# Turned rows as plain f32 matmuls, no folded row pairs, new instruction orders

## The chip, the core and the metric

The kernel runs on one core of one Trainium2 chip. The metric is device time of one execution in microseconds (us); the figure given is the median of three runs. The core's engines work at the same time and wait for each other by semaphores: TensorE (PE, matrix products, with its weight loads PEld), VectorE (DVE), ScalarE (ACT), GpSimd (POOL) and SyncE (SP, which here only issues DMAs). TensorE writes to PSUM, which has eight banks of 2 KB per partition; VectorE and ScalarE fetch results from there.

## What is computed

The input x has 2048 rows and 512 columns in bf16. Two layers with the same weights follow each other. Each adds a spectral filter, then a mixer with an MLP, both on normed rows:

```python
def _A_ref(x, w_r, w_i):
    X = rfft2(x);  X = X * (w_r + 1j * w_i);  return irfft2(X)
def _B_ref(x, w1, w2, w3, w4):
    h = gelu(layernorm(x) @ w1)
    # the four column quarters of h, shifted by +1, -1, +2, -2 rows
    x1 = x + concatenate([g0, g1, g2, g3]) @ w2
    return x1 + gelu(layernorm(x1) @ w3) @ w4

for _ in range(2):
    x = x + _A_ref(layernorm(x), A_w_r, A_w_i)
    x = x + _B_ref(layernorm(x), B_w1, B_w2, B_w3, B_w4)
return x
```

w1 and w2 are 512x512, w3 512x1792, w4 1792x512.

## The kernel before

x stays in on-chip memory as 16 tiles of 128x512, here called rows 0 to 15 (row q holds the rows p*16 + q of x, p being the partition). The transform over 2048 is split into one over p (128 points) and one over q (16 points); the transform over the 512 columns is another. All of them are matmuls with constant tables. Much of the work is in pairs of rows.

The order in which instructions are issued is written out by hand in three strings: ORDER_0 for the first front, ORDER_A and ORDER_B for the two layers. A token is one letter for an operation, a number, perhaps the engine that does it (A, V, P for ScalarE, VectorE, GpSimd; D is a product done by VectorE straight from PSUM), and after a dot the PSUM bank where its result begins. Every engine runs its own instructions in the order of the strings, and what stands behind a waiting instruction waits too. The steps that matter here:

- **First front** (ORDER_0). `s`: statistics of a row, on VectorE (one instruction), or for rows 1, 5 and 9 on ScalarE (two). `i`: their aggregate. `f`: the remaining arithmetic for a row that ScalarE did, on GpSimd; `f2` also issues four table loads (FL, TL twice, TR) from GpSimd's queue. `S` and `J`: root and reciprocal of the deviation for a group of rows, on ScalarE and VectorE. `Q`: the table T scaled by a row's factor. `O`: the transform over p of a pair of rows. `G`, `L`, `I`: fetching its result into V. After the last of them GpSimd copies the doubled planes of the filter W and makes a turned table.
- **Layer, spectral part.** `d`: transform over the columns, from all of V; `t` fetches it. `q`: transform over q; `x` fetches it; `p` multiplies with the filter. `b` (and `V`): back over q; `m` and `l` fetch into hT. `N`: VectorE negates a part of the table TR. `D` and `C`: back over the columns for a pair of rows m, into two banks; `Y` fetches a pair as bf16 (128x1024). `P`: back over p for one row; `a` adds it to x and sums the row.
- **Layer, norm and turn.** `s` squares (ScalarE), `r`, `e`, `i`, `M` make the factors, `n` norms a row (ScalarE, VectorE or GpSimd). `T` (and `U` for the second norm) turns a pair of rows with TensorE; `Z` (and `F`) fetches the turned rows into xT. `v`: product with w1; `h` its gelu; `u`: with w2; `f` the residual. `w`, `g`, `W`, `A`: product with w3, gelu, product with w4, addition. The second layer ends with stores `y`; the first runs the next front (`O` and what belongs to it) between its last products.
- `X`: a number of matmuls on zeros that nobody reads; `fill` makes them.

FOLD names row pairs whose way back over p is halved. For pairs 4 to 7 (rows 8 to 15), `K` fetches the right halves of the pair's result to f32, `H` (fold_D, line 670) makes sum and difference with the left halves on VectorE, and P then needs two matmuls of 256 columns (line 678) for the four (line 683) of the other rows:

```python
if q // 2 in FOLD[last]:
    for h in range(2):                                # 2 matmuls
        ...
for h, e, c in ((0, 0, 0), (0, 1, 0), (1, 0, 0), (1, 1, 1)):   # 4 matmuls
```

A turn writes eight transposes of 128x128 as bf16 into one bank, and the copy (line 154 on ScalarE, 152 on VectorE) fetches 128x1024 bf16.

Of the kernel before, what the change touches and what calls it, by code (L numbers as in the profile page):

```python
# [148 lines left out]

def copy(K, dst, src, eng):  # L150
    if eng == "V":
        K.nc.vector.tensor_copy(dst, src)
    else:
        K.nc.scalar.activation(dst, src, ACT.Copy, bias=0.0, scale=1.0)  # L154
# [406 lines left out]
def layer(K, last):  # L561
# [143 lines left out]

    def turn(key, rows):

        ps[key] = o = banks(K, 1)[:, 0].bitcast(BF16).rearrange("p (i t c) -> p i t c", i=2, t=4)
        for i in range(2):
            for t in range(4):  # L710
                nc.tensor.transpose(o[:, i, t], rows[:, i, t * P:(t + 1) * P], K.unit[:])  # L711
# [194 lines left out]
ORDER_A = """
d0.0 d2.4 t2A d6.2 d1.1 N0 t0V t6A t1V q0.6 q2.4 x2A d4.0 t4A q6.2 p0D q1.6 x1A d10.4 p2V d12.0 t10A t12A d8.6 q4.4
t8A q10.0 x10A p6D b6.2 m6A b2.7 d14.6 b7.3 q8.0 m2A p4D b4.4 t14A b5.2 x8A d15.5 q14.6 q12.0 m7A p10V b11.3 m5A t15A
m4A b3.2 p1V x14A b1.5 m1A b10.4 m10A p8V p12D q15.6 b8.5 m11A b9.4 b12.0 b13.1 m8A b0.3 p15D V12.5 m9A m12A b15.4 m3A
p14V m15A b14.7 m14A m13V V13.0 V14.1 V15.4 m0V l14V l13A l12V D2.6 D0.0 l15A C2 C0 Y0A D1.2 C1 D3.4 Y1A C3 P0.0 P1.2  # L910
Y2V Y3A P3.1 P2.3 P7.4 a0 s0 a1 s1 P6.0 a3 s3 D5.6 C5 P4.1 a2 s2 K5A P5.5 D4.2 a6 s6 a7 a4 r0 e0 a5 C4 s7 K4A i0 M0
n2P n3A s4 D6.4 D7.0 C7 n0P H5 H4 n1V s5 T1.6 Z1A r1 e1 P11.7 P8.2 T0.3 a11 i1 M1 n4P a8 Z0A C6 P10.6 P9.7 n6A v1.2 h1
a9 n5P T2.7 a10 n7P T3.6 s11 v0.2 K6V H6 Z3V P12.6 Z2A v3.4 K7V c1 c0 s9 P13.7 H7 P15.0 P14.1 s10 s8 h3 h0 r2 v2.4 n9P
n8P a13 a14 u0.1 h2 a12 n11V u3.3 n10V a15 T5.5 s12 s14 f3 s13 T4.0 s15 r3 n15P Z5V u2.2 n14P u1.7 c3 f2 E2P Z4A v5.3
k3 v4.5 T7.0 f0 f1 k1 h5 u4.1 n13V h4 c2 u5.4 k0 n12V T6.5 Z6A u6.2 f5 Z7V u7.4 f6 v6.6 v7.2 E3V f4 k2 E5V h6 E1V h7
u14.7 R0 o1V o2A E6V E0V o0V u12.1 o3V k4 f14 f7 k6 U0.2 k14 U1.6 F1V u15.0 E4V f15 u9.3 F0A w4.4 u8.0 g4 u13.7 k5 E7V
k7 R1 o5P w0.4 f8 E8V k8 f12 k12 o7P k15 E14V f13 k13 w3.0 g3 u10.2 f10 E12V w2.6 g2 f9 g0 k9 w1.0 g1 u11.7 f11 w5.2
k11 E11V k10 R3 E15V g5 o12P o14P R2 E10V w6.5 o4A g6 W2.2 E13V o15P U7.4 o10P U2.3 W3.0 o11P o13A A2 B2 j2 U5.7 A3
o6P U3.2 W1.5 A1 B1 F3A U6.2 F6A F5V E9P F2A W0.0 o9V A0 w7.2 F7A B0 j0 o8P U4.0 g7 w10.4 g10 B3 w9.2 w8.4 g8 F4V j1
w13.0 g13 j3 w17.4 g17 w14.0 g14 S0 Q3V Q0P Q1P g9 O0.4 G0A w11.6 g11 w12.1 g12 W5.0 A5 G0V I0P Q2A O1.2 B5 j5 W7.6  # L920
W6.1 A7 W4.4 A6 w15.0 B6 j6 G1A w16.6 G1V g15 w25.0 w18.2 g18 g25 A4 B4 I1P g16 w20.4 w19.2 B7 j7 j4 g19 g20 W10.1 A10
B10 j10 W9.5 S1 Q7A Q5A Q4A O2.0 Q6P O3.2 G3A G3V W8.4 A8 B8 j8 A9 B9 W11.3 A11 B11 G2A w22.4 G2V I2V I3V w23.2 w21.0
j9 j11 S2 Q11P Q10P g22 w24.4 Q8A g24 Q9A w26.6 g23 g26 g21 w27.4 O5.2 G5A O4.6 g27 G5V I5V G4A W12.0 A12 B12 G4V j12
S12 W15.1 A15 B15 j15 S15 J15 Q15V I4V W13.6 W14.3 A13 W24.7 B13 J12 j13 S13 J13 O15.1 A14 A24 B14 B24 j14 Q12A Q13P
S14 O6.4 G6A G15A J14 Q14V O14.6 G14A L15V L14A L6V
"""
ORDER_B = """
d15.3 t15V d1.2 d4.4 d0.3 t0V t1A q1.0 q15.6 t4A d12.2 q4.4 p1D x15A q0.6 t12A x4A d2.1 t2A p15V p0D b15.0 d10.3 t10A
m15V q12.6 x12A q2.0 d8.2 t8A p4V d6.4 d14.6 b1.7 p2D q8.2 t6A q10.0 p12V b4.4 t14A q6.5 m1A x10A b0.7 p8D x6A b2.1
b5.0 b12.5 b8.3 b9.2 m4A m5A b3.6 m2A p6V b7.4 m0A q14.0 m8A p10V m3A b6.7 b13.3 m7A b10.6 b11.4 m12A m6A V15.5 m9V  # L930
p14D b14.2 V14.7 V12.0 m10A m11V V13.1 m13A l14V m14A D0.2 l15A l12A l13A D2.5 C2 Y2V D1.0 C1 C0 Y0V Y1A D3.4 C3 Y3A
P4.7 a4 P5.1 P2.2 a5 s4 P7.3 s5 P6.6 a7 s7 P0.1 a6 s6 a0 P3.0 s0 a3 D5.4 C5 K5A P1.3 a2 D4.6 C4 r1 e1 s2 a1 D7.0 C7 i1
H5 X6.2 P10.2 K4A H4 M1 n6P s1 n7A T3.3 s3 P11.4 Z3A n4V n5P T2.6 r0 a10 P9.5 a11 e0 i0 D6.2 a9 K7V M0 P8.7 a8 n3P C6
Z2A s10 v2.4 n2A H7 T1.6 s9 K6V Z1V n0P n1P T0.7 H6 s8 s11 r2 v3.0 n10V n8V Z0A v1.6 n11V P14.2 a14 P13.3 a13 h3 T5.0
c0 P12.1 h2 h1 v0.4 P15.2 Z5V h0 u1.0 a12 n9V a15 T4.6 s12 Z4V u0.4 s14 f1 E1V s15 c1 s13 r3 n12P u2.5 f2 k2 f0 v4.2
v5.0 n15P u3.6 k1 n13A h4 n14V T7.7 f3 T6.2 h5 u4.3 k0 E3V E0V Z6V u5.6 Z7A f4 u7.1 v6.2 E2P k3 c2 f5 v7.6 f7 k7 h6 h7
u6.2 u13.0 f6 E7V R0 o1P o0A U0.1 F0V o2P u8.4 c3 f8 o3A U1.6 f13 E6P E13P E5V k6 k4 u9.5 f9 u14.4 F1A u15.0 f15 E9V
E4V f14 E14V k5 k8 R1 o4P u12.6 k13 w2.2 u11.7 f11 k9 g2 w4.0 k14 w1.2 w5.4 o7A k15 f12 w0.6 k12 R3 o14P o6V o13P g5
E11V g1 g4 w3.4 g3 w6.0 g0 E15V o15A u10.2 f10 k10 E12P U3.4 o12V E10P g6 W2.5 k11 R2 o5V U7.0 o11V U6.3 F6A o9P E8V
A2 W1.1 A1 F7A w23.6 w24.0 o8A U4.5 U2.2 F3A w27.3 g23 w22.6 F4A g24 F2V y2 w21.0 g22 o10P w25.6 g21 U5.2 F5V W0.1 g27  # L940
W3.0 A0 g25 w26.2 g26 W12.4 w8.6 W15.5 A3 w7.0 g7 A12 A15 W14.2 A14 w15.3 y0 W13.2 A13 w19.0 g15 g19 w20.4 w18.0 w13.2
g18 y1 g20 w16.0 g16 w14.4 y15 g8 g14 w17.0 w9.4 g9 w12.6 w10.4 g12 y3 g10 y12 y13 g13 w11.6 g11 W4.5 A4 y4 W7.3 W5.2
A7 y14 W6.6 A6 A5 y7 y5 y6 g17 W8.0 W11.6 A8 y8 A11 y11 W9.4 W10.3 A9 y9 A10 y10 W20.2 A20 y20
"""


# [28 lines left out]
```

## Time and profile before

| | |
|---|---|
| median of three runs | 357.88 us (357.71 to 357.96) |
| profiled execution: its own time, and its span | 357.88 us, 356.1 us |
| TensorE busy | 347.6 us in 2408 matmuls |
| VectorE, ScalarE, GpSimd busy | 181.6, 208.7, 102.7 us |
| first front: first product, last product | 8.48, 18.86 us |
| first layer: first D, first w1 | 37.93, 51.74 us |
| second layer: first d, first D, first w1 | 189.2, 207.34, 221.23 us |
| last product with w4 ends | 352.9 us |

Times in the profile are counted from the start of the span. Busy time of TensorE counts a matmul from start to modelled end, and matmuls overlap by their latency; so the step from one start to the next in a stream says what one costs. "Idle before" is the time that an engine stood still before the instructions of a group, with what ended it. In the chain that ended last, each piece is what the next one waited for.

### The profile page before, as it was taken

The numbers are of one execution on the slowest core, as the hardware profiler recorded it, in microseconds if no ns is written. First come the engines' busy times: TensorE is split into PE (matmuls) and PEld (weight loads), VectorE is DVE, ScalarE is ACT, GpSimd is POOL, SyncE is SP. The second block draws the span as 40 slices with busy tenths as digits, with TensorE's granted clock in tenths as the row PEclk, the third lists the DMA queues.
The fourth block names the chain that finished last, engine by engine and source line by source line (L and its number), as shares of the span: only waits on it lengthen the run. The fifth ranks groups of instructions, "written<-read, shape, count | busy, mean of one in ns | idle before, by whom it ended". The sixth has DMA issues, their size and how long they took to land.

```text
span 356.1 us, 6134 instructions
## 1 busy us (share of the span) xinstructions
PE 347.6 (98%) x2408; PEld 198.5 (56%) x2408; DVE 181.6 (51%) x399; ACT 208.7 (59%) x381; POOL 102.7 (29%) x213
## 2 busy tenths in 40 slices
...
GB/s 255 305 303 172 346 174 0 2 1 3 0 2 0 0 2 0 0 2 0 2 0 2 3 3 0 3 0 2 0 1 17 0 29 31 28 3 2 44 44 47
DMA packets 11534, 16.25 MB, mean 46 GB/s; under 512 B 1344, under 2 KB 8512, under 8 KB 11504
## 3 DMA queue, kind: packets, MB, share of 16 engines
...
q14 instruction: 11, 0.09, 0.1%
q10 hardware_dynamic: 144, 0.07, 0.1%
...
## 4 chain that ended last, share of the span: by engine, by line
PE 88%; DVE 5%; ACT 3%; issue 1%; DMA 1%; SPq 0%; ACTq 0%; DVEq 0%
PE ps L799 27%; PE ps L779 27%; PE ps L728 8%; PE ps L744 8%; PE ps L635 4%; PE ps L711 4%; DVE x_state L691 3%; PE ps L424 3%; PE ps L655 2%; PE ps L587 1%; PE ps L605 1%; DMA x_state<-in_A_x_dram 1%; DVE Y L670 1%; ACT TV L154 1%; PE ps L434 1%
## 5 line engine op out<-in xcount | busy, mean ns | idle before, releaser
L779 PE MATMUL ps<-xT,w 128*128 128x512 bf16 x448 | 99.6, 379 | 0.0
L799 PE MATMUL ps<-w,gT 128*128 128x512 bf16 (+2 forms) x476 | 99.5, 366 | 0.0
L786 ACT ACTIVATE gT<-ps 128x1024 bf16<-128x1024 f32 x56 | 55.3, 1023 | 73.5 <-PE ps L779 66.7
L805 DVE TENSOR_TENSOR x_state<-ps,x_state 128x512 bf16<-128x512 f32 (+2 forms) x34 | 22.3, 659 | 101.4 <-PE ps L799 99.4
L799 PEld LDWEIGHTS <-gT 128*128 128x128 bf16 x476 | 45.2, 98 | 49.7 <-DVE pairs L456 0.2
L779 PEld LDWEIGHTS <-w 128*128 128x128 bf16 x448 | 43.7, 98 | 52.1
L752 DVE SCALAR_TENSOR_TENSOR xn<-xn,ln_c,ps 128x512 bf16<-128x512 bf16 x32 | 23.3, 744 | 27.5 <-PE ps L744 18.3
L744 PE MATMUL ps<-w,hT 128*128 128x512 bf16 x128 | 30.6, 379 | 0.0
L728 PE MATMUL ps<-xT,w 128*128 128x512 bf16 x128 | 29.4, 379 | 0.5 <-ACT xT L154 0.5
L154 ACT ACTIVATE xT<-ps 128x1024 bf16<-128x1024 bf16 x19 | 19.0, 1019 | 12.4 <-PE ps L711 12.4
L298 ACT ACTIVATE junk<-xn 128x512 bf16<-128x512 bf16 x32 | 19.9, 622 | 4.8 <-DVE xn L752 4.5
L691 DVE SCALAR_TENSOR_TENSOR x_state<-ps,x_state 128x512 bf16<-128x512 f32 x32 | 20.5, 684 | 3.0 <-PE ps L678 1.5
L286 DVE BATCH_NORM_STATS2 ln_st<-x_state 128x6 f32<-128x512 bf16 (+2 forms) x30 | 19.4, 665 | 4.3 <-DMA x_state<-in_A_x_dram 3.9
L728 PEld LDWEIGHTS <-w 128*128 128x128 bf16 x128 | 12.4, 98 | 14.4 <-issue 0.7
L304 POOL TENSOR_SCALAR ln_mv<-ln_s 128x4 f32<-128x4 f32 x16 | 4.1, 258 | 55.8 <-DVE x_state L691 49.1
L298 ACT ACTIVATE xn<-x_state 128x512 bf16<-128x512 bf16 x32 | 19.8, 622 | 0.3
L744 PEld LDWEIGHTS <-hT 128*128 128x128 bf16 x128 | 12.2, 98 | 13.0
L711 PEld LDWEIGHTS <-xn 128*128 128x128 bf16 x256 | 16.1, 98 | 5.6 <-ACT xn L397 0.6
L711 PE MATMUL ps<-unit,xn 128*128 128x128 bf16 x256 | 18.2, 219 | 0.5 <-ACT xn L397 0.3
L735 ACT ACTIVATE hT<-ps 128x512 bf16<-128x512 f32 x32 | 17.2, 602 | 2.4 <-PE ps L728 2.3
L621 DVE TENSOR_TENSOR PB<-ps,W 128x1024 bf16<-128x1024 f32 x15 | 17.7, 1216 | 0.0
L635 PE MATMUL ps<-TR,PB 128*128 128x128 bf16 x256 | 16.3, 219 | 0.1
...
## 6 DMA issues: line engine op xcount, KB each, us to landing
...
```

What stands on the lines that cost most here:

```text
L154: K.nc.scalar.activation(dst, src, ACT.Copy, bias=0.0, scale=1.0)
L298: K.nc.scalar.activation(out, src, ACT.Square, bias=0.0, scale=D ** -0.5, accum_out=self.s[:, i, 1:2])
L635: nc.tensor.matmul(o[:, k0 * P:(k0 + 1) * P], lhsT=pab[u][:, k, 2 * (b - u) + h, f * P:(f + 1) * P], rhs=K.TR[:, k:k + 2, 2 * b + h], star ...
L691: nc.vector.scalar_tensor_tensor(K.x[:, q, :], ps.pop(("P", q)), 1.0, K.x[:, q, :], op0=ALU.mult, op1=ALU.add, accum_out=ln[g].s[:, i, 0:1])
L711: nc.tensor.transpose(o[:, i, t], rows[:, i, t * P:(t + 1) * P], K.unit[:])
L728: nc.tensor.matmul(o[:, i], lhsT=K.w1[:, t, j * P:(j + 1) * P], rhs=xT[g][:, :, t, :], start=(t == 0), stop=(t == 3))
L744: nc.tensor.matmul(o, lhsT=K.hT[:, j, st:st + P], rhs=K.w2[:, j, :], start=(j == 0), stop=(j == 3))
L752: nc.vector.scalar_tensor_tensor(xn[:, q, :], xn[:, q, :], ln[q // 4].c[:, q % 4:q % 4 + 1], ps.pop(("u", n)), op0=ALU.mult, op1=ALU.add, ...
L779: nc.tensor.matmul(o[:, i], lhsT=K.w3[:, c, t * P:(t + 1) * P], rhs=xT3[g][:, :, c, :], start=(c == 0), stop=(c == 3))
L786: nc.scalar.activation(gT[g][:, 2 * j:2 * j + 2, :], ps.pop(("w", k)), ACT.Gelu_apprx_tanh, bias=0.0, scale=1.0)
L799: nc.tensor.matmul(o, lhsT=gT[g][:, t, i * P:(i + 1) * P], rhs=K.w4[:, t, d], start=(t == 0), stop=(t == 13))
L805: nc.vector.tensor_tensor(x, ps.pop(("W", n)), x, op=ALU.add)
```

## The change

Three things change; all else, the loads among them, stays as it was.

1. The turn is a plain matmul with the unit matrix as moving operand. Its result is f32 over two banks in place of bf16 in one; one copy per pair of rows fetches 128x1024 f32.
2. FOLD is empty: rows 8 to 15 take the four matmuls as the others do, `K` and `H` are gone, and `Y` fetches pairs 4 to 7.
3. All three orders are new.

```diff
     def turn(key, rows):
 
-        ps[key] = o = banks(K, 1)[:, 0].bitcast(BF16).rearrange("p (i t c) -> p i t c", i=2, t=4)
+        ps[key] = o = banks(K, 2)
         for i in range(2):
             for t in range(4):
-                nc.tensor.transpose(o[:, i, t], rows[:, i, t * P:(t + 1) * P], K.unit[:])
+                nc.tensor.matmul(o[:, i, t * P:(t + 1) * P], lhsT=rows[:, i, t * P:(t + 1) * P], rhs=K.unit[:],
+                                 start=True, stop=True)
...
-        copy(K, to[g][:, 2 * h:2 * h + 2], ps.pop(key), eng)
+        copy(K, to[g][:, 2 * h:2 * h + 2].rearrange("p q t c -> p q (t c)"), ps.pop(key), eng)
...
-FOLD = [(4, 5, 6, 7), (4, 5, 6, 7)]
+FOLD = [(), ()]
 ORDER_0 = """
-s0 s2 s1 f0 s3 i2 s5 f2 i0 S0 i3 S1 s7 J0 s6 Q0A s4 s9 J1 Q1V O0.5 Q2A i6 i4 i7 S2 s10 J2 Q3A s11 f3 Q4A Q5A s8 i11
-i10 i8 s12 G0A S3 J3 s15 Q7A s13 Q10A Q9V i13 Q6P O1.2 Q8V O2.0 O3.4 i15 G2A Q11P i12 G1A s14 S4 J4 G3A i14 Q12V Q13V
-S5 O5.6 L5A O4.0 J5 G3V Q14P G5A G4A O6.2 Q15V I3V O7.6 O8.4 G6A G7A G8A L7V L8A L6V
+s1 f0 s0 i0 s2 i2 s3 i3 s8 s5 S0 J0 S1 J1 s9 s10 i8 s11 Q2A Q3A O1.6 i10 Q1A s12 i11 Q0P s15 f3 S3 J3 Q10A i12 s13 s4
+Q11A i13 s7 i4 Q8A O0.1 G0A s6 i6 S4 G1A J4 Q12V i7 Q9P O5.3 f2 L5A s14 S2 J2 Q4V Q7V i15 Q13A O4.0 Q6P O6.6 i14 Q5P
+G5V G4A S5 J5 L6A Q14V O3.4 G3A G6A O2.0 G2A Q15V O8.2 G8A L8A G3V I3V O7.6 G7A L7V
 """
 ORDER_A = """
-d0.0 d2.4 t2A d6.2 d1.1 N0 t0V t6A t1V q0.6 q2.4 x2A ...
+X5.0 d1.0 d0.1 t0A d2.2 t2A d10.6 t10A N0 t1V q0.4 q1.0 p0D ...
...
-... D2.6 D0.0 l15A C2 C0 Y0A D1.2 C1 D3.4 Y1A C3 P0.0 P1.2
-Y2V Y3A P3.1 P2.3 P7.4 a0 s0 a1 s1 P6.0 a3 s3 D5.6 C5 P4.1 a2 s2 K5A P5.5 D4.2 a6 s6 a7 a4 r0 e0 a5 C4 s7 K4A i0 M0
-n2P n3A s4 D6.4 D7.0 C7 n0P H5 H4 n1V s5 T1.6 Z1A r1 e1 P11.7 P8.2 T0.3 a11 i1 M1 n4P a8 Z0A C6 P10.6 P9.7 n6A v1.2 h1
+... D0.0 l12V D1.2 l13V l15A C0 C1 Y0A D3.4 C3 Y3A Y1V D2.6
+C2 Y2A P0.2 a0 s0 P3.3 a3 s3 P7.0 P2.6 a7 s7 P1.5 D5.2 a1 s1 P5.7 a2 s2 a5 D7.0 C7 Y7V D4.4 s5 P6.6 r0 e0 C4 i0 C5 M0
+a6 P4.7 a4 Y5V Y4A D6.0 n0V C6 s6 n1P P14.5 P8.4 P15.6 P9.7 s4 T0.2 Y6A P12.1 P13.0 a15 r1 e1 i1 n3A a9 a8 n2P T1.6
+a14 M1 n6P Z0A Z1A P10.2 a10 P11.3 a11 s8 s9 n7P s10 s11 n5V T3.4 Z3V a12 v1.6 h1 ...
...
 ORDER_B = """
...
-P4.7 a4 P5.1 P2.2 a5 s4 P7.3 s5 P6.6 a7 s7 P0.1 a6 s6 a0 P3.0 s0 a3 D5.4 C5 K5A P1.3 a2 D4.6 C4 r1 e1 s2 a1 D7.0 C7 i1
-H5 X6.2 P10.2 K4A H4 M1 n6P s1 n7A T3.3 s3 P11.4 Z3A n4V n5P T2.6 r0 a10 P9.5 a11 e0 i0 D6.2 a9 K7V M0 P8.7 a8 n3P C6
-Z2A s10 v2.4 ...
+... P5.5 P6.4
+P4.2 D4.0 Y1A P7.3 a5 s5 P2.5 D7.6 C7 a6 s6 a4 s4 P0.2 a7 P1.3 C4 s7 a2 s2 Y7V r1 P3.4 e1 i1 M1 D5.6 C5 Y4A P9.5 a0 s0
+P8.2 a3 a1 P15.3 s3 n5P n4P T2.0 a9 a8 s1 n6P Y5A r0 e0 D6.4 C6 n7V T3.6 Z3A Z2V i0 M0 n0V P14.2 P10.0 a10 n3P P11.1
+v3.6 ...
```

More of the change, by code (lines that the diff above doesn't have):

```diff
@@ L905 @@
+Q11A i13 s7 i4 Q8A O0.1 G0A s6 i6 S4 G1A J4 Q12V i7 Q9P O5.3 f2 L5A s14 S2 J2 Q4V Q7V i15 Q13A O4.0 Q6P O6.6 i14 Q5P
+G5V G4A S5 J5 L6A Q14V O3.4 G3A G6A O2.0 G2A Q15V O8.2 G8A L8A G3V I3V O7.6 G7A L7V
 """
 ORDER_A = """
-d0.0 d2.4 t2A d6.2 d1.1 N0 t0V t6A t1V q0.6 q2.4 x2A d4.0 t4A q6.2 p0D q1.6 x1A d10.4 p2V d12.0 t10A t12A d8.6 q4.4
-t8A q10.0 x10A p6D b6.2 m6A b2.7 d14.6 b7.3 q8.0 m2A p4D b4.4 t14A b5.2 x8A d15.5 q14.6 q12.0 m7A p10V b11.3 m5A t15A
-m4A b3.2 p1V x14A b1.5 m1A b10.4 m10A p8V p12D q15.6 b8.5 m11A b9.4 b12.0 b13.1 m8A b0.3 p15D V12.5 m9A m12A b15.4 m3A
@@ L910 @@
-p14V m15A b14.7 m14A m13V V13.0 V14.1 V15.4 m0V l14V l13A l12V D2.6 D0.0 l15A C2 C0 Y0A D1.2 C1 D3.4 Y1A C3 P0.0 P1.2
-Y2V Y3A P3.1 P2.3 P7.4 a0 s0 a1 s1 P6.0 a3 s3 D5.6 C5 P4.1 a2 s2 K5A P5.5 D4.2 a6 s6 a7 a4 r0 e0 a5 C4 s7 K4A i0 M0
-n2P n3A s4 D6.4 D7.0 C7 n0P H5 H4 n1V s5 T1.6 Z1A r1 e1 P11.7 P8.2 T0.3 a11 i1 M1 n4P a8 Z0A C6 P10.6 P9.7 n6A v1.2 h1
-a9 n5P T2.7 a10 n7P T3.6 s11 v0.2 K6V H6 Z3V P12.6 Z2A v3.4 K7V c1 c0 s9 P13.7 H7 P15.0 P14.1 s10 s8 h3 h0 r2 v2.4 n9P
-n8P a13 a14 u0.1 h2 a12 n11V u3.3 n10V a15 T5.5 s12 s14 f3 s13 T4.0 s15 r3 n15P Z5V u2.2 n14P u1.7 c3 f2 E2P Z4A v5.3
@@ L915 @@
[L915 to L924, printed above, removed]
@@ L925 @@
-S14 O6.4 G6A G15A J14 Q14V O14.6 G14A L15V L14A L6V
+X5.0 d1.0 d0.1 t0A d2.2 t2A d10.6 t10A N0 t1V q0.4 q1.0 p0D q2.2 d6.6 d14.4 x2A d15.5 q10.2 p1D t6A q6.0 t14A q14.6
+b0.4 x10A d12.2 x14A t15A d8.6 t12A b1.5 t8A m1A q12.2 p2V p6D p10V d4.0 m0V p12D b3.6 q8.4 t4A q15.0 m3A x8A b10.7
+b11.6 m10A x15A q4.4 b6.2 m6A b7.1 m11A b2.0 b12.2 m2A p8V b8.7 m12A b13.6 m13A p4D b9.3 m7A m9A V12.2 b5.6 b4.0 p14V
+b14.5 p15V b15.3 V14.1 m5A V15.4 m4A m15A m8V V13.7 l14A m14V D0.0 l12V D1.2 l13V l15A C0 C1 Y0A D3.4 C3 Y3A Y1V D2.6
@@ new lines @@
+C2 Y2A P0.2 a0 s0 P3.3 a3 s3 P7.0 P2.6 a7 s7 P1.5 D5.2 a1 s1 P5.7 a2 s2 a5 D7.0 C7 Y7V D4.4 s5 P6.6 r0 e0 C4 i0 C5 M0
+a6 P4.7 a4 Y5V Y4A D6.0 n0V C6 s6 n1P P14.5 P8.4 P15.6 P9.7 s4 T0.2 Y6A P12.1 P13.0 a15 r1 e1 i1 n3A a9 a8 n2P T1.6
+a14 M1 n6P Z0A Z1A P10.2 a10 P11.3 a11 s8 s9 n7P s10 s11 n5V T3.4 Z3V a12 v1.6 h1 n4P r2 n8P n9P c1 T2.2 Z2V v0.4 v3.2
+h0 a13 s13 n10V h3 v2.4 s15 T4.0 h2 s12 u0.7 n11V T5.2 Z5V Z4A u1.6 u3.5 s14 c0 f1 f0 v4.0 f3 h4 r3 n12P v5.2 n15A
+n13P n14V T7.0 u2.4 f2 T6.6 c3 h5 k3 u6.2 u5.3 c2 u7.4 u4.5 E3V k1 k2 Z7A Z6V k0 f5 E1V f4 R0 o1P v7.0 h7 u15.5 v6.0
@@ new lines @@
+f6 o3V E2V o2V U1.2 E0V o0V U0.6 F0V h6 u14.0 u9.1 f14 E5V F1A w2.6 f15 u13.0 f13 f7 k4 k7 u10.2 u11.3 f11 k6 E11V k5
+R1 o5P w0.4 E6V f9 g0 k9 E13V E7V w4.0 g4 f10 E15V k13 w3.4 g3 g2 u8.0 u12.3 f8 w1.5 o7V k14 E10P k10 k11 k8 R2 o10P
+w5.0 E4V g1 o6V g5 k15 f12 k12 E12P w6.2 o4V g6 W0.1 U3.2 F3A U2.6 W1.4 F2A E14V w9.2 g9 w7.6 E9V g7 A1 w10.4 g10 A0
+B0 w8.0 w12.2 o11A U5.4 E8P R3 g8 w11.6 w13.0 g11 W2.6 g12 o9V o8V g13 W5.7 j0 U4.0 B1 A2 W3.2 B2 o13A o12P j2 F5V F4V
+w15.0 W7.3 w20.4 g20 j1 A3 B3 j3 A5 o14V o15P S0 Q0P U7.6 B5 A7 Q1V j5 W4.2 g15 A4 B4 w17.0 g17 w19.2 g19 j4 w14.0
@@ new lines @@
+w16.2 W6.4 A6 B6 B7 j7 F7A g14 g16 U6.5 F6A Q3P j6 O0.0 G0A w18.2 g18 W10.7 A10 B10 S1 Q4V j10 Q2A W9.4 A9 G0V Q7A Q6P
+O1.2 W11.6 A11 B11 G1A w26.0 O3.4 G3A w21.6 G1V g26 I0P W8.2 A8 B8 g21 w25.0 G3V w27.2 g25 j11 w24.6 B9 j9 I1V j8 S2
+Q8P w22.0 Q9V Q5A Q10P g27 w23.2 O4.4 I3V g24 O2.6 g22 g23 W15.0 Q11A O5.2 G2A G2V I2V A15 B15 G4A j15 G5A G5V W13.6
+I5P A13 G4V S15 B13 J15 j13 W12.0 W14.7 I4P A12 S13 J13 B12 Q15V j12 S12 J12 Q13V W24.3 O15.0 Q12P O6.4 A14 A24 B14
+B24 j14 S14 L15A G15V G6A J14 Q14V O14.0 L6A L14A G14V
@@ L926 @@
 """
 ORDER_B = """
[L928 to L931, printed above, removed]
-P4.7 a4 P5.1 P2.2 a5 s4 P7.3 s5 P6.6 a7 s7 P0.1 a6 s6 a0 P3.0 s0 a3 D5.4 C5 K5A P1.3 a2 D4.6 C4 r1 e1 s2 a1 D7.0 C7 i1
@@ L933 @@
-H5 X6.2 P10.2 K4A H4 M1 n6P s1 n7A T3.3 s3 P11.4 Z3A n4V n5P T2.6 r0 a10 P9.5 a11 e0 i0 D6.2 a9 K7V M0 P8.7 a8 n3P C6
[L934 to L942, printed above, removed]
@@ L943 @@
-A7 y14 W6.6 A6 A5 y7 y5 y6 g17 W8.0 W11.6 A8 y8 A11 y11 W9.4 W10.3 A9 y9 A10 y10 W20.2 A20 y20
+d0.2 d1.0 t1V d15.4 d12.6 q1.0 t0A d4.2 p1D t15A t12A t4A q0.4 d2.6 q15.0 t2A p0D q4.2 q12.4 d6.6 x15V p4D d8.0 x12A
+q2.4 p2D t6A q6.6 t8A d10.2 x6A d14.0 b5.1 b0.6 t10A q8.4 m5A m0A q10.2 t14A b4.7 b1.1 b3.0 p15P b15.6 x10A m4A p6V
+b7.2 m1A b2.3 p8D b9.7 q14.4 b6.1 p10V m15A b10.6 m3A m2A b8.0 m7A m9A p12V b13.2 b12.3 b11.7 m10A V12.6 m6A p14D m12A
+b14.1 m8V V14.3 m14V V15.4 m13A l14V m11A V13.5 l13V D3.0 D0.2 l12A l15A C3 Y3V D2.4 C2 Y2A C0 Y0V D1.6 C1 P5.5 P6.4
@@ new lines @@
+P4.2 D4.0 Y1A P7.3 a5 s5 P2.5 D7.6 C7 a6 s6 a4 s4 P0.2 a7 P1.3 C4 s7 a2 s2 Y7V r1 P3.4 e1 i1 M1 D5.6 C5 Y4A P9.5 a0 s0
+P8.2 a3 a1 P15.3 s3 n5P n4P T2.0 a9 a8 s1 n6P Y5A r0 e0 D6.4 C6 n7V T3.6 Z3A Z2V i0 M0 n0V P14.2 P10.0 a10 n3P P11.1
+v3.6 a11 n2P s8 Y6A s10 a14 s14 s9 T1.0 n1V T0.4 a15 s11 r2 n10P v2.2 Z1V P12.0 Z0V h3 P13.1 v0.4 a13 s13 v1.6 h0 a12
+n11P h1 T5.0 h2 n8P u0.5 Z5V n9P T4.6 s15 u2.4 u3.0 Z4V v5.2 c1 s12 h5 f2 f3 k2 c0 f0 k3 u1.1 f1 r3 n12P n13V u4.7
+v4.2 T6.0 n14V n15A T7.4 h4 u6.6 Z6V k1 u7.2 u5.3 c2 f7 f6 Z7A v7.0 k0 h7 E0V v6.5 R0 o0A u15.2 h6 u14.0 E2V f4 E4V
@@ new lines @@
+o2A E1V E3V o3P U1.4 f14 k14 f5 E5V u11.1 o1P U0.6 F0V k4 f15 u12.3 u13.0 F1A w0.4 c3 k15 f13 f12 w3.2 k6 k13 u10.0
+f11 k12 k11 f10 u9.1 E11P w2.6 f9 k9 E9V w1.0 E6V k5 g3 E13V w4.2 g2 w6.6 k7 R1 g1 o4P g0 g4 o6V u8.0 f8 w5.2 g6 g5
+W2.0 W0.5 R3 o13P E12V o12A E7P E14V A2 y2 U6.0 E15V o15P k10 o14P U7.2 k8 R2 o5A o9P A0 o7V F7V W1.4 U3.2 U2.6 y0 F6A
+w21.0 F2A W3.5 E8V F3A g21 w26.0 g26 w24.2 w12.0 g24 o11A A1 g12 A3 w8.5 g8 w23.0 w22.2 w9.4 o8A g23 y3 g22 E10P w13.0
+g13 w25.2 w27.0 g27 g25 w7.6 g7 w10.0 o10A W13.7 A13 y1 g9 W15.3 A15 W12.4 U5.2 A12 w11.6 y15 g10 g11 U4.0 W14.5 A14
```

2 lines of the change are left out of this document (added).

## The prediction

> **What bounds the kernel now.** I read the busy shares first, then the stretches, then the chain that ended last between them. The profiled execution took 357.88 us, which is also the median of the three runs; its span is 356.1, so 1.78 us lie around the span and are taken as unchanged.
>
> ```profile
> PE 347.6 (98%) x2408; PEld 198.5 (56%) x2408; DVE 181.6 (51%) x399; ACT 208.7 (59%) x381; POOL 102.7 (29%) x213
> ```
>
> TensorE is the bound over the whole. The stretches (busy time of PE, PEld, DVE, ACT, POOL in each) say where it is not alone:
>
> ```profile
> 8.48:18.90 10.42, 10.29 (x120) 8.99 (x119) 9.85 (x35) 10.42 (x25) 7.10 (x13) 1.00 0.92 303
> 18.90:27.40 8.50, 7.29 (x90) 5.59 (x92) 7.48 (x10) 6.54 (x10) 5.42 (x8) 1.00 0.95 315
> 41.50:51.74 10.24, 9.29 (x90) 7.69 (x88) 9.30 (x28) 10.12 (x26) 4.11 (x13) 1.00 0.77 269
> 80.60:186.20 105.60, 105.60 (x578) 51.69 (x577) 43.13 (x101) 45.81 (x69) 25.06 (x42) 1.00 0.00 1
> ```
>
> In the long MLP stretch the array streams without a gap, so there each added matmul is paid in full and VectorE has room (43 of 106 us). Gaps lie in the first front, behind it, and in the stretch from 41.5 to 51.74, where the rows go back over p, are normed and turned. In that one the chain runs over VectorE and ScalarE:
>
> ```profile
> 37.93 3.61 PE ps L655 x32
> 41.53 0.45 PE ps L683 x4
> 42.70 4.03 DVE x_state L691 x14
> 48.24 1.28 DVE Y L670 x2
> 50.78 0.92 ACT xT L154
> 51.74 1.89 PE ps L728 x8
> ```
>
> **Prices.** The rows (busy, mean ns) for what the change touches:
>
> ```profile
> L683 PE MATMUL ps<-Y,Tinv 128*128 128x256 bf16 x64 | 7.7, 272 | 0.0
> L678 PE MATMUL ps<-Y,Tinv 128*128 128x256 bf16 x32 | 5.6, 272 | 0.3 <-DVE Y L670 0.3
> L670 DVE TENSOR_TENSOR Y<-ps,half 128x512 bf16<-128x512 f32 x16 | 10.0, 679 | 0.1
> L152 DVE COPY xT<-ps 128x1024 bf16<-128x1024 bf16 x13 | 8.9, 687 | 11.4 <-PE ps L711 11.3
> L152 DVE CAST Y<-ps 128x1024 bf16<-128x1024 f32 x3 | 3.7, 1224 | 2.4 <-PE ps L655 2.4
> L154 ACT ACTIVATE xT<-ps 128x1024 bf16<-128x1024 bf16 x19 | 19.0, 1019 | 12.4 <-PE ps L711 12.4
> ```
>
> A mean duration holds the array's latency; what counts in a stream is the step from start to start. The chain gives it: 4 matmuls of 256 columns in 0.45 us, 32 in 3.61, so 0.11 each.
>
> **The turn.** Part of the description changes nothing: the trace before shows 256 turns on TensorE (L711) and no DMA that transposes, and the diff leaves the load of W as it was. What is new is a plain matmul with an f32 result over two banks, for a bf16 result in one. On TensorE I price it at nothing: 16 turns take 0.89 us in the chain (53.62 to 54.52), 0.056 each, and the 16 plain 128-column matmuls of L434, f32 into two banks, take 0.89 too (155.81). The other plain row of that size, L635, takes 1.89 for 32, 0.059 each, which would be +0.9 for 256; the range keeps it, the sum takes the nearer row. [...] The result is dearer to fetch on VectorE alone: an f32 tile of this size costs 1.22 there (the Y row) for 0.69; ScalarE takes 1.02 either way (Y rows 1.023). The order has 16 such copies on VectorE, so 16 x 1.224 - 13 x 0.687 = +10.7 us. The folding that goes gives back 16 x 0.679 + 4 x 0.683 - 3 x 1.224 = 9.9. VectorE ends about 1 us heavier, hidden in its room in the MLP, but there is little cover before the first w1.
>
> **The fold.** Each of rows 8 to 15 goes back with four matmuls for two, in both layers: 64 added, 32 kept from before under another line, net 32 x 0.11 = +3.5 us of TensorE, 1.75 a layer. The six fill matmuls of the second layer go (-0.66); five come at the head of the first, where the array waits for V anyway (0.82 idle before the second product now). Without cover that would be 0.55.
>
> **The first front.** Before, ScalarE ran s1, s5, S0, S1 and Q0, and the first product started at 8.48, 0.56 after Q0 began at 7.92. In the new order s9 (8.34 to 9.56 in the trace, 1.22) stands ahead of the first scaling, Q2. S1 ends at 7.88, Q2 can begin at 9.1, the first product at 9.66: 1.18 later. The x loads still come first on SP's queue, so rows arrive as before. The front's products stream in about 9.7 (56 x 0.11, 64 x 0.056), so their end cannot be before 19.4; it was 18.86. GpSimd adds to this. f2, which issues four table loads, moves behind Q9; Q6 and Q5 queue behind those issues:
>
> ```profile
> 8.20 0.82 POOL L190 DMA_DIRECT2D FL<-tab_FL  x1
> 9.04 1.08 POOL L184 DMA_DIRECT2D TL<-tab_TL  x2
> 10.11 0.74 POOL L185 DMA_DIRECT2D TR<-tab_TR  x1
> 19.81 0.85 DVE L854 TENSOR_SCALAR TR<-TR 128x1024 bf16<-128x1024 bf16 x1
> ```
>
> With VectorE's statistics at 0.63 to 0.85 a row J3 comes at some 11.5, Q9 (0.93) ends at 12.5, f2 (three steps, 0.65) at 13.1, the issues (2.64) at 15.8, Q6 (0.63, waiting for J2) at 16.6, Q5 (0.93) at 17.5. Then the second half of O2, O8 and O7 at 0.67 each bring the last product to 19.5 to 20.1, and L7's copy (0.4) frees the second product of the first d at 20.4 to 20.8; before it ran at 20.04. I take **+0.75**, bounds +0.3 and +1.2. The TR load issued at 15.1 needs about the 7.2 us that such loads took, so it lands near 22.3, and N0 (0.85, DVE, shown above at 19.81) with t1 and p0 queued behind it may wait. p0 then starts between 23.1 and 24.0 for 22.77. VectorE's work from there to the first D is about as long as before (15.7), and TensorE's is the same, so part of the wait is absorbed: a further **+0.15**, bounds -0.4 and +1.0.
>
> **The way back, first layer.** From the first D to the first w1 took 51.74 - 37.93 = 13.8 us, with 12.3 of streaming (104 x 0.11: 64 in D, 32 and 8 in P; 16 turns at 0.056): 1.5 of waiting. The new order puts all 16 rows of P and three turns ahead of the first w1: 128 x 0.11 + 24 x 0.056 = 15.4. On VectorE, from the first a: six a at 0.61, Y7 1.15, two a, Y5 1.15, n0 0.32, a wait of some 0.7 for e1 (ScalarE has Y4 and Y6 ahead of it), a15 and a9, then turn 1 (0.45) and its copy (1.0): about 11.4, for 9.65 before. The first a comes 4.2 after the first D as before, so w1 15.6 after it, 0.2 of it waiting, and I add 0.3 at turns whose two banks await a copy. The term: 1.75 + 0.5 - 1.5 = **+0.75**, bounds +0.25 (all waits go) and +1.75 (none goes).
>
> **The way back, second layer.** Before, 13.95 from D (207.38) to w1 (221.33), 13.0 of streaming (104 x 0.11, 16 turns, six fills), 0.95 of waiting. New: 14 rows of P and two turns, 120 x 0.11 + 0.9 = 14.1 of streaming; VectorE's chain (five a, Y7, i1 behind e1, five a, n7, Z2 at 1.22) ends 9.9 after the first a, so at 14.1 too; 0.45 for waits where the two meet and behind. 1.75 - 0.66 + 0.45 - 0.95 = **+0.6**, bounds +0.1 and +1.1. The rest keeps its counts; its new orders get 0, bounds -0.3 and +0.8, since in some 266 us of gapless streaming a two-bank turn may meet a late copy.
>
> Sum: 0.75 + 0.15 + 0.75 + 0.6 = +2.25 on 357.88, **360.1 us**. About 0.2%, 0.7 us, is what a measurement of this kernel can tell from no change.
>
> **The rivals.** *The waits close* (faster): of TensorE's 344.4 us from 8.48 to 352.9 the streaming is about 337 (by columns of the moving tile: 512, 1124 x 0.216; 256, 360 x 0.11; 128, 732 x 0.056; 384, 28 x 0.16; L605, 128 x 0.068), so some 7.5 are waits. A denser order could close them, since plain P work stands ready earlier. Its places are the two ways back (1.5 + 0.95) and the stretches from d to b, which took 18.2 and 17.9 us for some 16.9 of streaming (32 x 0.056 + 32 x 0.11 + 64 x 0.068 + 128 x 0.057): 2.3 of waits. It decides from 3.5 recovered, where 3.5 - 0.66 is passed by the bound of 0.7. With the 2.45 and 1.8 of the others it gives 2.85 - 4.25 = -1.4, 356.5 us, if the front is no later. Against it stands the s9 ahead of Q2. Chance 0.09. *The matmuls hide and the front's delay is taken up* (no change): 2.85 - 2.45 = +0.4, 358.3, chance 0.07. *VectorE takes over* (slower still): f32 copies at 1.22 come late for w1, nothing of the waits goes, N0 waits for TR: 1.2 + 1.0 + 1.75 + 1.1 + 0.5 for the copies = +5.55, 363.4; for it speaks that VectorE was busy 9.3 of 10.24 in the way back, against it its room afterwards. Chance 0.2.
>
> **How the numbers follow.** My forecast has 0.64, slower by more than 0.2% with the last rival 0.84, same 0.07, faster 0.09. The bounds sum to about 0 and, with the 0.9 for turns, to +6.8; with not all at one end, 358.0 to 362.9 leaves out the faster rival and the outer part of the last one.
>
> **What would show it.** Right: first front product near 9.7, second product of the first d near 20.8, FL's issue near 13, 128 matmuls under the one line of P, 32 x 0.11 us more streaming, the first w1 near 54.4 and VectorE copies of xT at 1.22. Wrong: a first product still near 8.5; a first w1 no later than 52; gaps at w1 or w3 with a copy of xT as releaser (the last rival); turns that step faster than 0.056.

## The result and the profile after

The changed kernel takes 361.41 us (median of four runs, 361.04 to 362.46) for 357.92 of the kernel before (four runs): a ratio of 1.0102, 95% interval [1.0081, 1.0124]. The profiled execution took 361.43 us with a span of 359.7, so what lies around the span is 1.73 for 1.78. One point is needed to read the times below: besides executions whose mean granted clock is 0.998 to 1.000 ("at full clock" below) there are some at 0.995 or less, which in the kernel before took 1.7 to 2.1 us longer on average; the four of the changed kernel were at 0.990 to 0.995, while the four of the kernel before lay at 357.71 to 358.13.

The busy line of the page (busy time, share of the span, instructions):

```profile
PE 350.1 (97%) x2439; PEld 202.7 (56%) x2439; DVE 181.6 (50%) x388; ACT 209.2 (58%) x374; POOL 105.6 (29%) x215
```

TensorE is 2.5 us busier and the span 3.6 longer; VectorE's busy time is the same. The stretches say where that lies (PE, PEld, DVE, ACT, POOL, then granted clock, share of the DMA engines, GB/s): the first front, what stands behind it, the way back of the first layer up to the first w1, and the MLP.

```profile
9.73:21.30 11.57, 11.57 (x122) 10.39 (x122) 9.43 (x32) 9.42 (x20) 8.73 (x17) 0.85 0.85 245
21.30:30.00 8.70, 7.84 (x96) 5.91 (x95) 7.15 (x9) 7.01 (x11) 4.63 (x7) 1.00 0.93 339
44.80:56.58 11.78, 11.78 (x121) 10.62 (x119) 11.04 (x30) 11.44 (x26) 6.05 (x15) 1.00 0.40 130
84.00:189.00 105.00, 105.00 (x567) 51.01 (x566) 45.31 (x110) 46.37 (x70) 24.46 (x42) 1.00 0.00 1
```

In the third row PE is busy all the time (9.29 of 10.24 before): the waits of the way back are gone. The first row holds what the prediction did not have: a granted clock of 0.85 where it was 1.00. The chain that ended last confirms the third row. From the first D to the first w1 it runs over TensorE alone, where before it went over VectorE's additions and a copy of xT:

```profile
41.20 3.61 PE ps L655 x32
44.81 2.23 PE ps L683 x20
51.84 1.75 PE ps L683 x16
56.74 1.73 PE ps L729 x8
```

The groups for what was priced (busy, mean ns, idle before):

```profile
L683 PE MATMUL ps<-Y,Tinv 128*128 128x256 bf16 x128 | 16.5, 272 | 0.0
L711 PE MATMUL ps<-unit,xn 128*128 128x128 bf16 x256 | 18.5, 219 | 0.0
L152 DVE CAST xT<-ps 128x1024 bf16<-128x1024 f32 x16 | 19.4, 1218 | 10.3 <-PE ps L711 6.1 <-ACT xn L298 4.3
L154 ACT ACTIVATE xT<-ps 128x1024 bf16<-128x1024 f32 x16 | 16.1, 1021 | 11.0 <-PE ps L711 11.0
```

All of P is under one line. The turns cost what they cost before, 0.45 for eight in the chain. The f32 copies take 1.22 on VectorE and 1.02 on ScalarE, as priced.

Stage by stage, from the starts in the two traces:

| event | before | after | change |
|---|---|---|---|
| first product of the front (L424) | 8.48 | 9.73 | +1.25 |
| second product of the first d (L583) | 20.04 | 22.60 | +2.56 |
| p0 (L621) | 22.77 | 25.06 | +2.29 |
| first D (L655) | 37.88 | 41.15 | +3.27 |
| first w1 | 51.74 | 56.58 | +4.84 |
| second layer: first d | 189.22 | 192.87 | +3.65 |
| second layer: D | 207.34 | 210.74 | +3.40 |
| second layer: first w1 | 221.23 | 224.89 | +3.66 |
| span | 356.1 | 359.7 | +3.6 |

So 3.27 of 3.6 us are lost ahead of the first D. From there to the end it is 318.2 before and 318.5 after: 32 more matmuls, net of six fills, cost 0.3.

The clock dip lies at the start. The matmuls on zeros and the first products (start, duration, in brackets the idle time before), then PE's clock by windows of 1 us (third number from the end):

```profile
1.01 4.89 PE L269 MATMUL ps<-zeros 128*128 128x256 bf16 x30 [1.01 <-DVE zeros L260]
9.73 8.41 PE L424 MATMUL ps<-Tq,x_state 128*128 128x256 bf16 x80 [3.84 <-ACT Tq L407]
```

```profile
10.00:11.00 1.00, 1.00 (x15) 0.93 (x12) 1.00 (x4) 0.69 (x3) 0.39 (x2) 0.91 0.76 208
11.00:12.00 1.00, 1.00 (x9) 0.82 (x7) 1.00 (x5) 0.70 (x3) 0.47 (x1) 0.50 0.41 120
12.00:13.00 1.00, 1.00 (x9) 0.82 (x8) 1.00 (x4) 0.70 (x2) 0.84 (x3) 0.50 0.75 191
13.00:14.00 1.00, 1.00 (x8) 0.79 (x7) 0.96 (x4) 0.00 (x0) 0.99 (x2) 0.50 0.96 221
```

TensorE counts as fully busy there, with 9 matmuls a microsecond for 15. With the parts of the windows on both sides (0.91 there, 0.88 from 14 to 15) it was at half clock for 0.18 + 3 + 0.24 = 3.4 us, which loses 1.7 us of work. Only the clock column tells, the busy share doesn't.

### The profile page after: what moved, and what is told of

Read it like the earlier page. It is cut to its first block, busy times and chain, and to the rows that moved or that the text cites. A ratio compares the mean times of both kernels' runs of the same rounds, so it can differ in the third digit from the quotient of the medians.

```text
span 359.7 us, 6165 instructions
## 1 busy us (share of the span) xinstructions
PE 350.1 (97%) x2439; PEld 202.7 (56%) x2439; DVE 181.6 (50%) x388; ACT 209.2 (58%) x374; POOL 105.6 (29%) x215
## 4 chain that ended last, share of the span: by engine, by line
PE 91%; ACT 4%; DMA 2%; DVE 2%; issue 1%; ACTq 0%
PE ps L800 27%; PE ps L780 27%; PE ps L729 8%; PE ps L745 8%; PE ps L711 4%; PE ps L683 4%; PE ps L655 4%; PE ps L635 4%; PE ps L605 2%; ACT TV L154 1%; PE ps L587 1%; PE ps L424 1%; DMA x_state<-in_A_x_dram 1%; ACT V L154 1%; DMA T<-tab_T 1%; PE ps L434 1%
## 5 line engine op out<-in xcount | busy, mean ns | idle before, releaser
L753 DVE SCALAR_TENSOR_TENSOR xn<-xn,ln_c,ps 128x512 bf16<-128x512 bf16 x32 | 23.0, 744 | 14.2 <-PE ps L745 13.0
L152 DVE CAST xT<-ps 128x1024 bf16<-128x1024 f32 x16 | 19.4, 1218 | 10.3 <-PE ps L711 6.1
L736 ACT ACTIVATE hT<-ps 128x512 bf16<-128x512 f32 x32 | 18.0, 599 | 9.2 <-PE ps L729 9.1
L154 ACT ACTIVATE xT<-ps 128x1024 bf16<-128x1024 f32 x16 | 16.1, 1021 | 11.0 <-PE ps L711 11.0
L286 DVE BATCH_NORM_STATS2 ln_st<-x_state 128x6 f32<-128x512 bf16 (+2 forms) x30 | 19.6, 661 | 4.7 <-DMA x_state<-in_A_x_dram 4.4
L621 DVE TENSOR_TENSOR PB<-ps,W 128x1024 bf16<-128x1024 f32 x17 | 19.9, 1217 | 2.1 <-PE ps L605 1.9
L729 PEld LDWEIGHTS <-w 128*128 128x128 bf16 x128 | 12.4, 98 | 14.0 <-DVE xT L152 0.2
L711 PEld LDWEIGHTS <-xn 128*128 128x128 bf16 x256 | 16.5, 98 | 5.1 <-ACT xn L397 0.2
L745 PEld LDWEIGHTS <-hT 128*128 128x128 bf16 x128 | 12.2, 98 | 12.7
L711 PE MATMUL ps<-unit,xn 128*128 128x128 bf16 x256 | 18.5, 219 | 0.0
```

The costliest lines, as they stand in the source:

```text
L621: nc.vector.tensor_tensor(t[:, :, 2 * i:2 * i + 2], o[:, :, i * 256:(i + 1) * 256].unsqueeze(1).to_broadcast([P, 2, 2, 256]), K.W[:, :, 2 ...
L711: nc.tensor.matmul(o[:, i, t * P:(t + 1) * P], lhsT=rows[:, i, t * P:(t + 1) * P], rhs=K.unit[:], start=True, stop=True)
L729: nc.tensor.matmul(o[:, i], lhsT=K.w1[:, t, j * P:(j + 1) * P], rhs=xT[g][:, :, t, :], start=(t == 0), stop=(t == 3))
L745: nc.tensor.matmul(o, lhsT=K.hT[:, j, st:st + P], rhs=K.w2[:, j, :], start=(j == 0), stop=(j == 3))
L753: nc.vector.scalar_tensor_tensor(xn[:, q, :], xn[:, q, :], ln[q // 4].c[:, q % 4:q % 4 + 1], ps.pop(("u", n)), op0=ALU.mult, op1=ALU.add, ...
```

## The experiments

**Which part costs: the orders.** Three kernels exchange whole stages. One takes the changed kernel with the old front, one the kernel before with the new front, and one the changed kernel with the old order up to the first D.

```diff
 # e2: changed kernel           # e6: kernel before
-ORDER_0 = new                  -ORDER_0 = old
+ORDER_0 = old                  +ORDER_0 = new
 # e8: changed kernel
-ORDER_0, ORDER_A to "D0.0" = new
+ORDER_0, ORDER_A to "D0.0" = old     # then "D0.0 D1.2 l15A C0 C1 Y0A", the rest new
```

> The kernel after with the first front's order of the kernel before; the layers' orders, the empty FOLD and the f32 turns stay. Theory (the loss is made before the first D, by the front's order): the second product of the first d comes near 20.0 in place of 22.6, and the time falls by 2.6, by 3.3 if the 0.7 that the d to b stretch lost came from the front too: 358.1 to 358.8 us, 1.001 to 1.003 of before. Rival (the 32 more matmuls, 2.85 us net of fills, are the price, and the front's delay is taken up behind it): not below 360.7 us, 1.008.

Measured: 361.26 us, ratio 1.0071 [1.0047, 1.0096]; its three executions at full clock took 359.99 to 360.12. The first product came at 8.89, but the first D at 41.12; this profiled execution had the clock at 0.50 from 9 to 12, which is part of that. TensorE waited for a table that is loaded late (total, count, longest):

```profile
PE ps L605 <- DMA TL<-tab_TL: 0.8, 1, 0.8
```

The old front doesn't take the loss away: at full clock 2.1 us of it are left, so the new spectral order loses by itself.

> The kernel before with the first front's order of the kernel after; layers, FOLD and turns stay as before. Theory (late front, and with it the late table loads, cost the time): the first product comes at 9.3 to 9.9, TR lands at 22.3 to 22.8 and N0, which stands ahead of VectorE's first fetches of d in this order too, waits for it; the first product with the filter near 25 in place of 22.8 and the time +2.0 to +2.5, ratio 1.006 to 1.007. Rival (the first layer's order costs the time, the front is taken up): below +0.7, 1.002.

Measured: 360.43 us, ratio 1.0061 [1.0037, 1.0084]. The new front alone costs 2.5 us by the medians and 2.0 in the profiled execution, which was at full clock (359.97 us, first D at 39.96). Behind the front VectorE waits at N0 for the table TR:

```profile
DVE TR L854 <- DMA TR<-tab_TR: 2.6, 1, 2.6
```

> The kernel after with the orders of the kernel before up to the first D: the whole first front and the first layer's transform, filter and way back over q. From the first D on (32 more matmuls, f32 turns, new orders of both layers, no fills) it is the kernel after. Theory (the whole loss lies ahead of the first D): +0.3 on before, ratio 1.001. Rival (the added matmuls and turns cost what they weigh): +2.8, 1.008.

Measured: 358.52 us, ratio 1.0019 [0.9998, 1.0040]; first D at 38.26, and from there to the end 318.3. Turns, fold and both new ways back together cost 0.1 to 0.3 us; the rest of the change's loss is in the order ahead of the first D.

**The turn by itself.**

```diff
-    nc.tensor.matmul(o[...], lhsT=rows[...], rhs=K.unit[:], start=True, stop=True)   # f32, two banks
+    nc.tensor.transpose(o[:, i, t], rows[...], K.unit[:])                            # bf16, one bank
```

> The kernel after with the turns of the kernel before (transposes into one bf16 bank); FOLD and all orders as after. Theory (the turn's form is no part of the loss): 16 turns still take 0.89 us on TensorE, VectorE's 16 copies fall from 1.22 to 0.69 us each, and the time stays within 0.3 us of 361.4. Rival (f32 copies on VectorE come late for the products that wait for them): 360.4 us or less. [...]

Measured: 361.50 us, ratio 1.0079 [1.0051, 1.0108]. L711 has 219 ns and eight turns 0.45 us in the chain, with a granted clock of 1.00, the same as plain matmuls; VectorE's copy of xT falls to 685 ns from 1218, which doesn't show in the time, since nothing waited for it. From the first D to the end it is 318.4 for 318.5. The dearer copies (19.4 us on VectorE for 10.9 here) were fully covered, and the rival that VectorE takes over is out.

The profiled execution of this run, 359.87 us, was at full clock, so it also shows the new orders without the dip. The first product came at 9.25 and the second product of the first d at 20.11, hardly later than before, yet the first D came at 39.69, +1.81. From the one to the other it took 19.58 us for 17.84, with these waits on the way:

```profile
DVE TR L854 <- DMA TR<-tab_TR: 1.9, 1, 1.9
DVE PB L621 <- DMA W<-W: 1.3, 1, 1.3
```

**The added matmuls by themselves.**

```diff
-FOLD = [(4, 5, 6, 7), (4, 5, 6, 7)]
+FOLD = [(), ()]                      # kernel before; in the orders K becomes Y, H goes
```

> The kernel before with FOLD empty alone: rows 8 to 15 take four matmuls, each K is a Y on the same engine, each H is left out; bf16 turns and all else of the orders stay, the six fills too. 32 matmuls of 256 columns more, 3.5 us. Theory (the ways back have waits that take them up, since VectorE loses 16 sums of 0.68 us there): +0.3 to +1.0 on before, ratio 1.001 to 1.003. Rival (each added matmul is paid): +3.5, 1.010.

Measured: 363.23 us, ratio 1.0141 [1.0103, 1.0179], 361.3 to 361.8 at full clock. From the first D to the end 321.9 for 318.2, that is +3.7, where 32 x 0.11 = 3.5: in the old order the added matmuls cost their full weight, and the array still waits at turns of that order:

```profile
PE ps L711 <- ACT xn L397: 1.5, 2, 1.0
```

The same matmuls cost 0.3 in the new orders. This run's rival was right. The gain of the new orders from the first D on is thus about 3.4 us, 0.66 of it from the six fills that they leave out, and it pays for the fold's removal.

**The walls ahead of the first D, one by one.** Three kernels take the changed kernel and move what the one before showed as late; a fourth loads a table early behind the old front.

```diff
 # e3:  ORDER_0   -... J1 s9 s10 i8 s11 Q2A Q3A O1.6      +... J1 s10 i8 s11 Q2A Q3A s9 O1.6
 # e7:  e3, and ORDER_A   -... t10A N0 t1V ... p1D t6A    +... t10A t1V ... p1D N0 t6A
 # e10: e7, and ORDER_0   -... s8 s5 S0 ... O5.3 f2 L5A   +... s8 s5 f2 S0 ... O5.3 L5A
 # e9:  e2, and the load of TL2 moved from load_rest (L201) behind load_TR in load_tables
```

> The kernel after with one token moved in the front: s9, row 9's statistics on ScalarE, goes from ahead of the first two scalings to behind them. Theory: the first product comes near 8.5 (for 9.73), the array's idle time falls to about 2.6 us, the clock stays at 1.00, and the time falls by 2.5, to 358.9 us (1.003). Rival (the later tables set the front's end): the first product comes near 8.5, but the front ends within 0.5 us of 21.1 and the time falls by less than 0.6. If only the start counts and not the clock: -1.2, 360.2 us.

Measured: 361.09 us, ratio 1.0064 [1.0042, 1.0086]. The first product came at 8.79 and the second product of the first d at 20.70, two microseconds sooner than in the changed kernel. This profiled execution, at full clock, took 360.21 us, which is what the expectation gave for the earlier start alone; six of the eight had 0.995 or less. Behind the front N0 waited:

```profile
DVE TR L855 <- DMA TR<-tab_TR: 2.2, 1, 2.2
```

> The kernel after with s9 behind the first two scalings and N0 moved on VectorE from ahead of t1 to behind p1, so that nothing before the second product with the filter waits for the TR load. Theory (behind the late first product stands the late TR load, which held N0 for 2.2 us when s9 alone was moved): the first product with the filter comes near 23.0 in place of 24.3, the first D near 38.7, and the time falls by 2.5 from the kernel after, ratio 1.003. Rival (the W and TL loads behind it are a third wall at the same place): the first product with the filter comes earlier, the first D not before 39.7, and the time stays within 0.4 us of the run with s9 alone, ratio 1.006.

Measured: 361.27 us, ratio 1.0086 [1.0058, 1.0115]. N0 no longer holds p0 up, but p0 still started at 24.29, now for the doubled planes of W, as the rival had it:

```profile
DVE PB L621 <- DMA W<-W: 2.2, 1, 2.2
```

> The changed kernel with s9 behind Q2 and Q3 and N0 behind p1 as in the run before it, and now f2 with its four table loads right behind s5, as in the kernel before. Theory: late loads of the tables, and the doubling of W that queues behind them, were the wall that was left (p0 24.29, waiting 2.2 for W). Then FL is issued at about 8, p0 starts at 23.0 to 23.4, the first D at 38.2 to 39.0 and the median is 358.5 to 359.5. Rival: the doubling of W and TL2 stand behind the last scaled tables on GpSimd and not behind the loads, so p0 stays past 24 and the first D past 39.5, median 360.2 to 361.4.

Measured: 361.11 us, ratio 1.0098 [1.0068, 1.0128], 360.8 to 361.4 at full clock; p0 at 24.75, first D at 40.84 (this execution had the clock at 0.50 from 9 to 12). The theory fell. No wait for a load is left behind the front, but the issues now stand on GpSimd ahead of f3, and ScalarE's S3 waits 1.35 us for it, so the front itself ends later:

```profile
12.11 0.30 ACT L386 ACTIVATE ln_r<-ln_mv,eps 128x4 f32<-128x4 f32 x1 [1.35 <-POOL ln_mv L382]
```

From the second product of the first d to the first D it takes 18.55 us, exactly as in the changed kernel, for 17.84 before: with every table in time, 0.7 stays with the new spectral order.

> The changed kernel with the first front of the kernel before, as in the run with the old front, and now with the load of the turned table TL2 issued with the other table loads, ahead of the front's end (there it was issued at 22.42, and TensorE waited 0.8 us at L605 for that table, its weight loads 1.0). Theory: the new spectral order takes planes of the upper half early, and its loss with the old front (first D at 41.12 for 37.88 in the kernel before) is this load. Then no wait for TL stands at L605, the first D comes between 38.0 and 38.7, and the median is 358.3 to 358.9. Rival: the loss is in the order itself, in the waits of VectorE for the products at L605 and of the array for ScalarE's copies. Then the waits for TL go and the first D stays at 39.5 or later in an execution at full clock, median 359.8 to 361.2.

Measured: 359.27 us, ratio 1.0029 [1.0003, 1.0055]; 358.8 to 359.3 at full clock, where the run with the old front had 360.0. The wait for TL is gone, and the first D comes at 38.69 in this execution, whose first product was early (8.13). From the second product of the first d to the first D it is 18.90 for 19.63. So the load was a wall, but its removal is worth 0.7 us here of the 2.1 that the run with the old front had lost. The rest of the distance to the 41.12 of that run is no gain of the load: 0.76 come from the earlier first product and 0.94 from the dip that only that execution had. The median stays above what the theory gave. The next load now holds p0, a plane of W, though p0 starts at 22.30, ahead of the 22.77 of the kernel before, so this wait isn't shown to be what is left:

```profile
DVE PB L621 <- DMA W<-in_A_w_i_dram: 1.3, 1, 1.3
```

**The clock.** Three kernels change the number of matmuls on zeros at the start.

```diff
-WAKE = 30
+WAKE = 45     # e1: changed kernel
+WAKE = 38     # e11: the kernel of e8    e12: kernel before
```

> The kernel after with 45 instead of 30 matmuls on zeros ahead of the first product, all else as it is. In the kernel after the array stood idle for 3.84 us (5.90 to 9.73) and was then granted half its clock from about 10.9 to 14.2. Theory (that half clock costs time to the end): with the idle time under 3 us the clock stays at 1.00, the front's last product comes 1.6 us earlier, and the time falls by 1.6, to 359.8 us (1.005 of before). Rival (the front waits for its scaled tables anyway, from VectorE and GpSimd): the clock stays up but the time falls by less than 0.4, to 361.0 or more.

Measured: 360.97 us, ratio 1.0072 [1.0050, 1.0094]. Eight of 13 executions were at full clock, at 360.1 to 361.6 (median 360.4), four of them at 360.1 to 360.3. That is 1.0 less than the changed kernel's 361.41, between the theory and the rival. That the clock stays up with an idle time under 3 us was the author's estimate, and no run shows such a limit: it fell after 2.13 us in the run with early f2 and stayed at 1.00 after 3.66 in the one with the new front alone. In the profiled one the front stayed at 1.00 and brought the second product of the first d at 20.62. Behind it TensorE waited 2.9 us for a late TL, and there the clock fell, to 0.50 from about 28.6 to 35.5, so the times behind that are not used:

```profile
29.60 2.10 PE L605 MATMUL ps<-TV,TL 64*128 64x256 bf16 x18 [2.93 <-DMA TL<-tab_TL]
28.00:29.00 1.00, 0.00 (x0) 0.00 (x0) 0.00 (x0) 0.00 (x0) 0.00 (x0) 0.82 1.08 373
35.00:36.00 1.00, 1.00 (x14) 0.86 (x13) 0.41 (x1) 0.74 (x2) 0.00 (x0) 0.77 0.74 216
```

> The changed kernel with the order of the kernel before up to the first D, and with 38 matmuls on zeros at the start for 30. Theory: the low granted clock behind the start, which lengthened some executions by 1.2 to 2 us, comes from the array's idle time ahead of the first product (2.31 us there); eight more matmuls shorten it by 0.4 to 0.9 us. Then the first product stays near 8.66, fewer than one run in six shows 0.995, and the median falls from 358.5 to about 357.9 to 358.2, the same as the kernel before. Rival: the clock falls whatever the idle time; the share of such runs and the median (358.5) stay. Should the fills still run at 8.5, the first product is late and the median rises above 358.8.

Measured: 358.26 us, ratio 1.0000 [0.9984, 1.0016], 357.99 to 358.69, all 12 executions at full clock, where with 30 it was eight of 12. In the profiled one the first product came at 8.96, after 1.39 us of idle time.

> The kernel before with 38 matmuls on zeros at the start for 30. Theory (idle time ahead of the first product lets the clock fall): nothing later than 8.6 for the first product, fewer runs at a clock of 0.995 than of the kernel before on the same chip, median lower by 0.1 to 0.6 us. Rival: the idle time is not what decides; the median stays within 0.2 us, or the fills reach into the first product's time and it rises by 0.3 or more.

Measured: 357.89 us, ratio 1.0003 [0.9990, 1.0016], 357.65 to 358.77, all 12 at full clock. Of the kernel before with 30, 20 of 71 executions beside these experiments were at 0.995 or below. The 29 of them that ran beside this experiment had a median of 357.93 as well, but reached 361.43. Over all executions here the mean falls from 358.41 to 358.03: the median stays, as the rival had it, and the long executions are gone, as the theory had it. At full clock alone the added fills gain nothing (358.03 on average for 357.76). By the mean this is the best version of the study; none has a median clearly below the kernel before.

## Why the prediction was right in its number and not in its parts

The time lies in the range and on the predicted side, 1.3 above 360.1, but two errors of opposite sign meet in it, and one cause was missing. That the sum without the missing cause comes out at 360.2, next to the forecast, is luck.

- **First front, +0.75.** Its steps came as worked out: first product 9.73 for 9.66, FL issued at 13.18 for 13.1, TR at 15.09 for 15.1. At full clock the second product of the first d comes at 20.62 (45 matmuls on zeros) and 20.63 (new front, old layers), within the 20.4 to 20.8 predicted: +0.6. With bf16 turns, where the first product came at 9.25, it was 20.11. In the changed kernel it came at 22.60. The step that failed is that the front's products stream at 0.11 and 0.056: at half clock they don't. This was in no term, since every stretch of before showed 1.00, and the sum took the later first product as a delay alone, not as 3.84 us of idle array.
- **From d to b, +0.15 with bounds to +1.0.** This is the term most out of size. Second product of the first d to first D: 17.84 before; 19.2 to 19.6 with the new front at full clock (the runs with s9 behind, N0 moved, the old layers behind it, and bf16 turns), so +1.3 to +1.7; 18.55 in the changed kernel, +0.7. The wait of N0 for TR was named, with a landing near 22.3, where N0 began at 22.8 and 23.1 behind its waits of 2.2 and 2.6; "part of the wait is absorbed" was the error. W's doubling, TL2 and W's own load stand right behind TR, and the new order needs them early.
- **The clock and the load waits share time.** In the changed kernel no transfer is waited for behind the front, because the dip has already made everything late; at full clock the same orders wait for TR and W (the run with bf16 turns). So the dip costs less than its 1.7, about 1.3: the sum at full clock is 357.9 + 0.6 + 1.4 + 0.3 = 360.2, which is where half of the full-clock executions with 45 matmuls on zeros lie (the run with bf16 turns: 359.87, from +0.07, +1.74 and +0.19); with the dip it is +2.56, +0.71 and +0.3, the measured 3.6.
- **Ways back, +0.75 and +0.6.** The distances from D to w1 were right: 15.43 for 15.6, 14.15 for 14.1. What was too large are the 0.5 and 0.45 for new waits: there are none. From first D to the end of the layer +0.24 in the first (148.28 to 148.52) and +0.27 in the second (145.57 to 145.84), at the lower bound given for the first, +0.25, and between bound and term for the second, +0.1 and +0.6; 0.1 each came back ahead of the second D and behind the last addition. "First w1 near 54.4" was missed by 2.2, all of it from ahead of D.
- **Turns and copies.** The price of nothing on TensorE was right, and the bf16 turns show it directly: among other products they take 219 ns each and 0.45 us for eight in the chain, at a granted clock of 1.00, like the plain matmuls. The kernel before shows the same 219 ns, and 1.00 in every stretch with turns.
- **Rivals.** "The waits close" was half right: of the 2.85 of added matmuls net of fills 0.3 are left, so the new ways back recover about 2.5 us, all of its 2.45. The 1.8 that it took from d to b did not come: that stretch lost 0.7 in the first layer and gained 0.25 in the second. "If the front is no later" was its condition, and that failed too. "VectorE takes over" is out: no gap at w1 or w3 has a copy of xT as releaser on PE. "The matmuls hide" held from the first D on, but the front's delay was not taken up.

What stays open: why the new spectral order takes 0.5 to 0.7 us more from the first d to the first D when all loads are in time. No run separates its parts. In three of the four profiled dips the place was the first front, in the fourth the wait for TL; for executions without a profile only the mean clock says that they had one. The runs with more matmuls on zeros shorten the idle time and lengthen the work ahead of it at once, so which of the two keeps the clock up is open as well.
